# A new order of the same steps for a fused long convolution and feed-forward kernel

## The chip, the cores and the metric

The kernel runs on one core of a Trainium2 chip. The metric is device time in microseconds (us); the engines are PE (matmuls), DVE and ACT (elementwise work and copies out of PSUM), POOL and SP (here mostly queues that issue DMAs).

## The reference

```python
x = A_q                                   # (1, 2048, 640) bf16, as k and v
xn = layernorm(x)
k_shift = sum(k_pad[:, t:t+S] * shift_k[:, 3-t] for t in range(4))   # 4 taps
kv = k_shift * v
y = irfft(rfft(kv, 4096) * rfft(ssm_k, 4096))[:2048] + kv * ssm_D    # along the sequence
s = xn * y
g = silu(gelu(xn @ w1 + b1) @ w2 + b2)    # 640 -> 1728 -> 640
out = x + s * g
```

## The kernel before

The 2048 positions lie as 128 partitions by 16 rows of 640 channels. SBUF holds one pool, `mem`, of 111 rows of 128 x 640 bf16, and every intermediate result sits in rows that are given by number. PSUM's eight banks are given by number too.

The whole kernel is a list of some 990 short words, `PLAN`. Each word is one step: a name with its indices, then `/row` for where its result goes in `mem`, `@bank` for its PSUM bank (`@6.7` takes two), and `~a` or `~d` for the engine of a copy out of PSUM (ACT or DVE). The program runs through the words and emits each step's instructions; each engine, and each engine's DMA queue, then executes its own in the order of the words. Waits between engines are put in from the rows and banks that steps share. So the order on an engine is the order of the list, and a step that is not ready holds all that follows it there. At most eight DMAs of SP's queue are under way: each waits for the landing of the one eight places before it, and POOL's likewise.

The steps, with their lines:

- Feed-forward, in four chunks `c` of 512 positions: `st`, `rs`/`sq`, `nm` are the layer norm (L405 to L421); `tx`, `tt` turn x on PE (L426, L432) and `te` copies it out (L191 on ACT, L192 on DVE, as all steps with `~a` or `~d`); `ha`, `hb`, `h` are the first matmul (L451, five matmuls), `he` the gelu (ACT, L456); `g` is the second matmul (L466, 14 matmuls of 320 columns), `ge` the silu (ACT, L471), `gm` the product with xn (DVE, L475). `wu` and `wv` are matmuls on nothing that warm PE (L267).
- Convolution: both filter and kv go through a transform in two stages. Filter: `kt` turns it (L483), `kc` copies it out, `kf` is the first stage (two matmuls, L197), `ke` copies it out, `ks` stores it to DRAM as scrK (POOL, L496). kv: `cm`, `ca`, `cv` are the taps, their sum and the product with v (DVE, L502, L505, L508), `uf` the first stage (L197), `ue` its copy, `us` its store to scrU (POOL, L518). The stage between goes through DRAM, since it regroups the lines: `fl` loads from scrK (SP, L521; it needs all 16 `ks`), `ff` is the second stage in 32 x 32 pieces (L207), `fe` its copy, `mk` a copy with partitions swapped (SP, two DMAs, L532). `ml` loads from scrU (SP, L535; it needs all 16 `us`), `mu` is its second stage (L207), `mp` the product of the spectra (DVE, L544), `mc` and `md` the first inverse stage (L207), `me` its copy, `ms` the store to scrC (POOL, L558).
- Sine tables: `ws`, `ss` (ACT); `it` turns them (L563), `ie` copies them out.
- Last stage: `yl` loads from scrC (SP, L576; it needs all 16 `ms`), `y` is the last inverse stage (four matmuls, L583), `yc` its copy (ACT, L587), `yt` the gate (DVE, L592), `yo` adds x (DVE, L598), `os` stores the output (SP, L603).
- Input loads, all on SP: `xl` and `q` (x), `wa` (w1), `wb` (w2), `cl` (filter), `kl` and `klh` (k), `vl` (v).

Of the kernel before, what the change touches and what calls it, by code (L numbers as in the profile page):

```python
# [41 lines left out]
ca0_3 ks3 kt7@3 ge0_6/2 cm1_3/39 kt10@4 kc7/12~a kf5_1@6.7 kf5_0@0.1 cv0 kc10/60~a g0_3@5 gm0_6 ke5_0/63~d ke5_1~a
cm1_2/61 ks5 kt9@4 ge0_3/0 kt6@2 cm2_0/58 kc9/107~a kf7_0@0.1 kf7_1@6.7 ke7_0/6~a gm0_3 g0_5@3 ca1_1 kc6/14~a
cm3_0/85 ke7_1~a ca1_2 uf0_0@4.5 ks7 ge0_5/1 uf1_0@0.1 kt8@2 ue0_0/41~a cm2_1/101 uf1_1@6.7 g0_4@3 ue1_0/12~a ca1_3
ue1_1~a st2_1 us1 uf0_1@4.5 cv1 ge0_4/2 kf6_0@0.1 kf6_1@6.7 ue0_1~a st2_0 g0_2@3 kc8/110~a us0 ke6_0/4~a st2_3
ke6_1~a uf3_1@4.5 ca2_1 ge0_2/0 uf2_0@0.1 ks6 uf2_1@6.7 ue2_0/67~a kt11@2 cm2_2/61 kt12@3 ue2_1~a uf3_0@0.1 st2_2
# [5 lines left out]
h1_3@2 ke12_1~d ke14_0/0~a kc13/107~a it3@3 ca3_2 ks12 uf5_1@0.1 he1_3 kf13_0@4.5 cm4_0/39 h1_7@7 ue5_1~a ca3_3
ke13_0/108~a us5 kf13_1@0.1 ca4_1 he1_7 it2@6 kf15_0@4.5 ke13_1~a cv3 h1_12@2 ke15_0/6~a ks13 cm4_2/41 ie2/43~a
uf6_0@0.1 uf6_1@4.5 gm0_7 h1_4@7 cm4_3/12 ue6_0/19~a ue6_1~d ie3~a h1_10@6 cm5_1/21 us6 he1_4 uf7_1@0.1 cm5_0/23
uf7_0@4.5 he1_10 h1_9@3 ca4_2 ue7_0/25~a ue7_1~a ca5_1 kf15_1@6.7 kf14_1@4.5 he1_9 h1_8@0 us7 ca4_3 ke14_1~a
cm5_2/27 ke15_1~a h1_11@1 ks14 cv4 he1_8 ks15 h1_5@3 he1_12 ca5_2 he1_11 cm5_3/2 uf8_0@4.5 he1_5 uf9_0@6.7 cm6_2/4
# [25 lines left out]
gm2_0 me18/33~a ml14/51 mp19/12 mu20@2.3 mu24@6.7 he3_0 h3_4@5 mp20/103 mc19@0.1 md19 mp24/95 he3_4 mu22@2.3 h3_3@4
me19~a mp22/85 ms9 mc20@0.1 mu23@6.7 md20 he3_3 h3_13@5 me20/87~a mp23/59 mc21@2.3 mc22@0.1 md21 he3_13 md22 h3_8@4
me21~a me22/53~d ms10 mu31@6.7 mc23@2.3 he3_8 gm2_7 md23 mu28@0.1 h3_1@5 mp31/68 me23~a ms11 mc24@2.3 md24 mp28/39
he3_1 mu25@6.7 h3_12@4 me24/70~a mp25/72 mu27@2.3 mu26@0.1 h3_5@5 he3_12 mp26/27 mc25@6.7 md25 he3_5 h3_11@4 me25~a
mp27/31 ms12 mc26@0.1 mu29@6.7 md26 he3_11 h3_6@5 me26/85~a mp29/33 mc27@2.3 mu30@0.1 md27 he3_6 h3_2@4 me27~a
# [581 lines left out]
```

## Time and profile before

| | us |
|---|---|
| median of 3 runs | 208.4 (208.17 to 208.75) |
| profiled execution, its own time | 207.69 |
| its span (first to last instruction) | 205.9 |
| PE busy | 192.1 |
| DVE busy | 175.8 |
| ACT busy | 159.7 |
| POOL busy | 39.8 |

The span is what the profile's rows divide up; the time of the execution has 1.8 us around it. PE's granted clock was 1.00 throughout. PE's bounds are its own work and the idle time between: with 93% busy, the waits ahead of its matmuls tell more than its busy time. In a list of waits the columns are the total, how often, and the longest; in a chain, the start, the duration and what ran; in a timeline, start, duration, engine, line and operation.

### The profile page before, as it was taken

What the parts mean: (1) busy time and instruction counts of PE and PEld (TensorE: products, weight loads), DVE (VectorE), ACT (ScalarE), POOL (GpSimd) and SP (SyncE); (2) the same over time, 40 slices, a digit from 0 to 9 for tenths busy, and PEclk for the clock granted to TensorE, in tenths of its full rate; (3) what the DMA queues carried; (4) which work ended last, traced back from release to release, by engine and by line L of the source; (5) the groups of instructions that cost most, each with busy time, mean ns of one, the idle gap of its engine ahead of it and who ended that gap; (6) DMA issues with size and microseconds to landing.
All of it is one profiled execution on the core that took longest, in us unless ns stands there. A gap on an engine that the chain in (4) does not pass through costs nothing.

```text
span 205.9 us, 5536 instructions
## 1 busy us (share of the span) xinstructions
PE 192.1 (93%) x2194; PEld 114.1 (55%) x2194; DVE 175.8 (85%) x300; ACT 159.7 (78%) x246; POOL 39.8 (19%) x71
## 2 busy tenths in 40 slices
PE   2989999999989999999999999999999999999982
PEld 1576666677656655656753333566653333666750
DVE  8999559799999999999897797899799997036983
ACT  5899999568999999987799777754688767645760
POOL 8302003212361323210240002111221212100000
PEclk9999999999999999999999999999999999999999
DMA  6999999994454435699997999999971323599993
GB/s 223 371 411 295 361 363 416 410 426 176 191 199 183 172 149 193 184 381 400 316 351 251 309 378 371 368 357 394 338 241 43 131 81 119 173 302 389 337 338 121
DMA packets 27120, 57.71 MB, mean 280 GB/s; under 512 B 2966, under 2 KB 16983, under 8 KB 27094
## 3 DMA queue, kind: packets, MB, share of 16 engines
q1 hardware_dynamic: 23072, 41.62, 57.6%
q0 software_dynamic: 3840, 15.73, 19.8%
q8 instruction: 17, 0.28, 0.6%
q14 instruction: 9, 0.07, 0.1%
q10 hardware_dynamic: 182, 0.01, 0.1%
HBM read 33.76 MB, written 18.35 MB: 253 GB/s over the span
## 4 chain that ended last, share of the span: by engine, by line
PE 54%; DMA 18%; DVE 12%; ACT 11%; issue 3%; SPq 1%; ACTq 1%; DVEq 0%
PE ps L451 22%; PE ps L466 16%; DMA mem<-scrK 8%; PE ps L207 7%; DMA mem<-scrC 6%; PE ps L197 5%; DMA scrK<-mem 3%; DVE mem L502 3%; DVE mem L505 3%; DVE mem L192 2%; ACT mem L191 2%; ACT hT L456 2%; DVE stats L405 2%; ACT L456 1%; ACT mem L587 1%
## 5 line engine op out<-in xcount | busy, mean ns | idle before, releaser
L451 PE MATMUL ps<-mem,w_sb 128*128 128x512 bf16 (+1 forms) x310 | 69.1, 363 | 0.1
L466 PE MATMUL ps<-w_sb,hT 128*128 128x320 bf16 x448 | 66.0, 299 | 0.3 <-ACT mem L191 0.3
L191 ACT CAST mem<-ps 128x640 bf16<-128x640 f32 x94 | 62.3, 699 | 3.1 <-PE ps L207 1.6
L466 PEld LDWEIGHTS <-hT 128*128 128x128 bf16 x448 | 42.7, 98 | 19.2 <-issue 2.4
L544 DVE TENSOR_TENSOR mem<-ps,mem 128x1280 bf16<-128x1280 f32 x32 | 46.0, 1485 | 3.5 <-PE ps L207 1.7
L456 ACT ACTIVATE hT<-ps,b_f 128x512 bf16<-128x512 f32 (+1 forms) x56 | 37.3, 694 | 10.8 <-PE ps L451 10.4
L451 PEld LDWEIGHTS <-w_sb 128*128 128x128 bf16 x310 | 28.4, 99 | 27.8 <-issue 4.9
L192 DVE CAST mem<-ps 128x640 bf16<-128x640 f32 x34 | 27.6, 820 | 8.7 <-PE ps L207 3.0
L471 ACT ACTIVATE sl<-ps 128x320 bf16<-128x320 f32 x32 | 13.9, 438 | 21.2 <-PE ps L466 20.8
L502 DVE TENSOR_TENSOR mem<-mem 128x1280 bf16<-128x1280 bf16 x32 | 25.4, 818 | 1.2 <-DMA scrK<-mem 1.2
L197 PE MATMUL ps<-mem 128*128 128x320 bf16 x128 | 23.7, 299 | 1.4 <-ACT mem L191 0.7
L207 PE MATMUL ps<-mem,mats 32*32 32x320 bf16 x1024 | 22.8, 300 | 1.2 <-DMA mem<-scrK 0.4
L558 POOL DMA_DIRECT2D scrC<-mem x16 | 11.4, 716 | 59.3 <-ACT mem L191 32.6
L191 ACT COPY mem<-ps 128x640 bf16<-128x640 bf16 (+2 forms) x27 | 20.6, 783 | 1.5 <-PE ps L426 0.8
L207 PEld LDWEIGHTS <-mats 32*32 32x32 bf16 x1024 | 9.6, 88 | 17.7 <-issue 14.7
L505 DVE TENSOR_TENSOR mem<-mem 128x1280 bf16<-128x1280 bf16 x24 | 19.2, 810 | 0.0
L475 DVE TENSOR_TENSOR mem<-mem,sl 128x320 bf16<-128x320 bf16 x32 | 9.7, 318 | 8.2 <-ACT sl L471 8.2
L197 PEld LDWEIGHTS <-mem 128*128 128x128 bf16 x128 | 12.0, 98 | 8.3 <-issue 2.5
L496 POOL DMA_DIRECT2D scrK<-mem x16 | 9.1, 569 | 33.9 <-DVE mem L192 21.2
L518 POOL DMA_DIRECT2D scrU<-mem x16 | 8.7, 545 | 32.6 <-ACT mem L191 19.1
L405 DVE BATCH_NORM_STATS2 stats<-mem 128x6 f32<-128x320 bf16 x32 | 13.8, 474 | 0.0
L587 ACT CAST mem<-ps 128x640 bf16<-128x640 f32 x16 | 10.1, 705 | 2.0 <-PE ps L583 1.7
(75 smaller groups left out, 138.5 us busy)
## 6 DMA issues: line engine op xcount, KB each, us to landing
scrK<-mem POOLq DMA_DIRECT2D x16, 320.0 KB, 4.2
scrU<-mem POOLq DMA_DIRECT2D x16, 320.0 KB, 3.5
mem<-scrK SPq DMA_DIRECT2D x16, 320.0 KB, 4.3
mem<-mem SPq DMA_DIRECT2D x32, 160.0 KB, 5.5
mem<-scrU SPq DMA_DIRECT2D x16, 320.0 KB, 6.6
scrC<-mem POOLq DMA_DIRECT2D x16, 320.0 KB, 4.2
mem<-scrC SPq DMA_DIRECT2D x16, 320.0 KB, 6.2
mem<-in_A_q_dram SPq DMA_DIRECT2D x7, 640.0 KB, 7.5
```

Of the source, the lines that this page charges most:

```text
L191: return nc.scalar.copy(out=out_ap, in_=in_ap)
L192: return nc.vector.tensor_copy(out=out_ap, in_=in_ap)
L197: nc.tensor.matmul(out=o[:, h, :], lhsT=lhsT, rhs=rhs[:, h * HALF:(h + 1) * HALF], start=start, stop=stop)
L207: nc.tensor.matmul(out=o[j, h, :], lhsT=m[i, i], rhs=rhs[i, h * HALF:(h + 1) * HALF], start=start, stop=stop)
L405: nc.vector.bn_stats(out=stats[:, n, h, :], in_=x_row(n)[:, h * HALF:(h + 1) * HALF])
L451: nc.tensor.matmul(out=bank(hname(c, ft))[:, a:b], lhsT=w1_sb[:, t, ft * P:(ft + 1) * P], rhs=rhs, start=(t == 0), stop=(t == DT - 1))
L456: nc.scalar.activation(out=hT[0:M, ft, :], in_=bank(hname(c, ft))[0:M, :], func=ACT.Gelu_apprx_tanh, bias=b1_f[0:M, ft:ft + 1], scale=1.0)
L466: nc.tensor.matmul(out=bank(f"g{c}_{i}")[:, 0:HALF], lhsT=hT[0:M, ft, q * P:(q + 1) * P], rhs=w2_sb[0:M, ft, hs], start=(ft == 0), stop=(f ...
L471: nc.scalar.activation(out=at["sl", c, i], in_=bank(f"g{c}_{i}")[:, 0:HALF], func=ACT.Silu)
L502: nc.vector.tensor_tensor(out=rows(f"cm{i}_{j}", 2), in0=rows("kz0", 2, 3 + 2 * i - j), in1=taps(j), op=ALU.mult)
L505: nc.vector.tensor_tensor(out=rows(f"cm{i}_0", 2), in0=rows(f"cm{i}_0", 2), in1=rows(f"cm{i}_{j}", 2), op=ALU.add)
L544: nc.vector.tensor_tensor(out=rows(f"mp{g}", 2).rearrange("p k (h c) -> p k h c", h=2), in0=banks(f"mu{g}")[:, None, :, :].to_broadcast([P ...
```

## The change

The same steps stand in a new order. The new order was found by moves within the old one, judged over replays in which the lengths of transfers were varied. The list keeps every step; rows and banks are given out anew, 46 of the copies out of PSUM change between ACT and DVE, and the one step `wv2` (two warm-up matmuls) becomes `wv1` twice. No function changes. All 63 lines of the list differ; these are the ones with the steps that the prediction speaks of (the old lines, then the new ones):

```diff
-io1/0 dm qs xl0_0/8 xl0_1 id pd/12 cl0/19 wa0 cl4 qr xl1/35 wa2 w cl1 io2 wu@0 kz0/39 cl3 st0_0 ws1/58 cl2 mh st0_1
-klh pt@1 em0@2 pb sq0 em1@3 kz1 rc0 nm0_0 nm0_1 tx0@4 st0_2 tx1@5 wa1 te0_0/65~a wv2 st0_3 te0_1~a ee0/69~a wb0
-ha3@6 ee1~d ha0@7 sq1 ws2/73 rc1 ha2@1 nm0_2 nm0_3 ha1@0 wb1 st1_0 em3@4 tx2@5 em2@2 st1_3 tx3@3 st1_1 te0_3~a
-ws0/77 it1@3 kl0 te0_2~d st1_2 hb2 hb1 xl3/81 ee3~d he0_2 rs1 hb0 s it0@5 hb3 kl3 h0_12@4 he0_3 he0_0 kl2 h0_13@1
...
-ke0_0/61~d h0_7@0 kc2/63~a he0_12 kf2_0@6.7 tt1_0@1 he0_7 ke2_0/13~d xl2/15 kf1_1@2.3 vl2/93 h0_8@4 te1_0/97~d
-te1_1~a ke1_1~d kf0_1@6.7 he0_8 h0_9@5 vl1/0 cm1_1/4 ks1 ke0_1~a cm0_3/6 kt4@4 ks0 he0_9 kf2_1@0.1 kt3@2 cm0_1/101
...
-gm0_0 ge0_1/1 kf4_0@4.5 cm0_2/58 kf3_1@0.1 ke4_0/101~a kf4_1@6.7 g0_6@2 gm0_1 ca0_2 ke4_1~a ke3_1~a kc5/110~d ks4
...
-ue3_0/39~a kf8_1@6.7 us2 ca2_2 ue3_1~a rs2 kf8_0@0.1 ke8_0/63~a gm0_2 kf9_0@4.5 ke8_1~d ke9_0/108~a kf10_1@0.1 gm0_5
-kf10_0@6.7 kc12/14~a cm2_3/87 ks8 kf9_1@4.5 ke10_0/6~a us3 tt1_2@3 nm2_1 ca2_3 te1_2~a g0_7@6 ke9_1~a nm2_2 nm2_3
...
-uf8_1@0.1 h1_6@2 ue9_0/87~a ca5_3 ue8_0/47~a fl0/33 uf9_1@6.7 ue8_1~d fl10/107 he1_6 h1_13@3 fl6/31 ue9_1~a cv5
-fl2/29 us8 fl1/85 tt2_0@2 he1_13 us9 cm6_3/58 fl3/60 uf10_0@4.5 uf11_0@0.1 te2_0/62~a cm6_0/41 uf11_1@6.7 g1_2@3
...
-fl11/0 te2_1~a fe10/109~d us15 mk4/19 nm3_1 fe11~a nm3_3 nm3_0 mk5/58 ff14@6.7 ff5@4.5 ff18@0.1 ge1_7/2 nm3_2 h2_0@3
-fe14/33~a fe5~d fl8/41 fe18/60~a gm1_7 mk2/105 ff19@6.7 ff15@4.5 he2_0 h2_11@2 fe19~d fl13/103 fe15~d fl14/12
-ff21@0.1 ml0/23 ff20@6.7 ml2/53 he2_11 h2_9@4 fe20/55~d ml8/68 fe21~a ml7/101 ff22@2.3 ff24@6.7 he2_9 ff23@0.1
...
-h2_6@5 mk12/21 me1~d me2/95~a ms0 mc3@2.3 mc4@6.7 md3 he2_6 md4 mu5@0.1 h2_10@4 me3~d ml5/51 me4/87~a mp5/107 ms1
...
-me16/27~a ml12/19 tt3_1@4 te3_0/0~a mc14@0.1 md14 mp17/87 mc15@2.3 mk13/6 md15 me14/101~a tt3_2@5 me15~a mu18@0.1
...
-h3_10@4 me30/87~d me31~a h3_7@5 ms15 he3_10 he3_7 g3_2@4 yl15/21 g3_5@5 ge3_2/2 yl13/41 yl14/6 yl4/109 yl10/4
...
-yc11 yo12_1 g3_3@0 yl1/66 yo2 yc8 yt10 os2 yt11 yl6/68 yo10 yt8 y0@6.7 os10 ge3_3/0 yo11 y9@2.3 yc0 yo8 os11 y7@4.5
-gm3_3 os8 yc9 yt0 g3_0@1 yo13_1 yc7 yt9 os13 yo0 yt7 os0 yo9 y5@6.7 ge3_0/2 yo7 os9 y1@2.3 gm3_0 yc5 os7 yo12_0
-y6@4.5 yc1 os12 yt5 g3_6@0 yc6 yo5 yt1 os5 yt6 yo1 yo6 ge3_6/1 os1 os6 gm3_6 yo15_0 os15_0
+io1/0 dm qs xl0_0/8 xl1/12 id pd/16 xl0_1 wa0 wa2 qr cl0/23 cl1 w cl2 io2 wu@0 kz0/39 cl3 st0_0 ws1/58 mh cl4 st0_1
+pt@1 em0@2 wa1 pb sq0 em3@3 kz1 rc0 wv1 nm0_0 nm0_1 tx0@4 st0_2 tx1@5 te0_0/65~a em1@6 klh st0_3 te0_1~a wv1
+ee0/69~a ha2@7 ee1~d ha0@1 sq1 ws2/73 rc1 ha1@0 nm0_2 nm0_3 tx2@2 tx3@6 kl0 te0_2~d ha3@4 te0_3~d st1_0 hb3 wb0 hb2
+ws0/77 st1_1 hb1 h0_13@5 wb1 st1_3 h0_11@2 he0_1 st1_2 xl2/81 h0_10@6 s rs1 kl1 he0_11 h0_12@0 he0_3 he0_2 it0@2
+vl0/85 it1@4 he0_10 hb0 d he0_13 nm1_1 kt1@7 nm1_3 he0_12 kt0@6 nm1_2 em2@5 nm1_0 he0_0 vl1/89 kc1/58~d tt1_0@0
...
+ha4@4 he0_6 kc0/16~d ha5@3 cm0_2/63 hb4 kc2/17~d hb5 cm0_1/101 ke1_0/103~a kf0_0@6.7 h0_8@5 he0_5 cm0_0/105
...
+cm0_3/101 he0_7 kl3 kt3@1 kc8/58~d vl2/65 kt4@4 he0_9 kf2_1@6.7 sm kf0_1@2.3 ke2_1~a ca0_2 g0_0@5 kc3/39~a vl3/0
...
+ke7_1~a cm2_2/6 ge0_3/1 uf1_1@2.3 ks7 ca2_1 uf1_0@6.7 kf6_0@4.5 ks1 cm2_3/101 g0_2@1 ue1_0/63~a ue1_1~a ca2_2
...
+ke10_1~a kf11_1@4.5 uf4_0@2.3 he1_0 ke11_1~d h1_1@6 ue4_0/109~d ks11 kf12_0@0.1 uf5_0@4.5 ks0 ca3_2 kt13@2 he1_1
...
+he1_11 fl0/91 cm6_2/89 fl6/30 h1_13@2 he1_6 fl4/32 gm0_5 fl1/42 ue8_0/109~d uf8_1@4.5 fl3/6 he1_13 uf11_0@0.1 fl2/26
...
+ge1_6/0 cv7 ue12_1~a uf13_1@0.1 st3_2 ff6@4.5 us12 ff7@6.7 g1_3@2 ue13_1~a us11 fe6/22~a st3_0 us8 fe7~a us10 gm1_6
...
+rs3 uf15_1@4.5 ue15_0/0~d tt2_2@7 tt2_1@6 ue15_1~a ff10@2.3 te2_2~d ff11@0.1 ff8@4.5 te2_1~d g1_7@7 fe10/52~a us13
+gm1_1 fe11~a fe8/93~d us9 nm3_2 us15 nm3_3 ff9@2.3 ff14@0.1 ff5@4.5 nm3_0 ge1_7/1 h2_0@6 fe9~a fe14/2~d fe5~a
+ff18@2.3 ff20@0.1 he2_0 mk2/6 ff19@4.5 h2_11@7 fe18/105~d fe20/91~d fl13/54 ff15@2.3 mk4/89 fe19~d he2_11 ff21@0.1
+h2_9@6 fe15~a ml0/18 fe21~d ml2/109 nm3_1 ff24@4.5 ml1/79 ff23@2.3 ff22@0.1 he2_9 h2_5@7 fl15/77 fe24/75~d fe22/73~a
...
+mu28@4.5 mu31@0.1 md23 h3_1@2 mp28/105 ms0 me23~a ms2 he3_8 h3_5@6 mp31/109 he3_1 ms4 ms9 mu25@4.5 mc24@2.3 md24
...
+me31~a gm2_7 he3_9 h3_7@2 gm2_6 ms15 he3_10 he3_7 g3_4@3 yl15/6 g3_2@2 yl4/85 yl13/24 yl14/26 yl3/0 yl12/28 g3_5@0
...
+yc4 y14@4.5 yc13 yl5/4 yt4 g3_7@2 yt15 yc14 yo4 yl1/16 ge3_4/2 yt14 yt13 yl6/105 y3@6.7 gm3_2 gm3_4 ge3_7/0 y12@0.1
...
+yc7 yt0 os11 yt9 os15_1 yt7 yo9 y5@2.3 yo7 ge3_0/1 os9 y1@0.1 yo0 os8 yc5 gm3_0 y6@6.7 os0 yo13_1 yc1 yt5 os13
+g3_6@4 yc6 yo5 os7 yt1 os5 yt6 yo1 yo6 ge3_6/0 os1 os6 gm3_6 yo12_0 yo15_0 os15_0 os12
```

In the old order the stores `ks`, `us`, `ms` stand where their data is ready, and loads of scrK, scrU and scrC are spread among the steps that use them. In the new one many of the stores stand later (`ks1`, `ks0`, `ks2`; `us8`, `us10`, `us11`, `us13`, `us9`; `ms0` to `ms7`), and many loads earlier (`kl0` ahead of `wb0`; `fl4`, `fl8`, `fl12`, `fl14`; `ml9`, `ml14`, `ml15`; all `yl` ahead of all `os`). `yo12_0` and `os12` move to the very end.

More of the change, by code (lines that the diff above doesn't have):

```diff
@@ L42 @@
[L42 to L46, printed above, removed]
@@ L52 @@
[L52 to L56, printed above, removed]
@@ L82 @@
[L82 to L86, printed above, removed]
@@ new lines @@
+ke0_0/107~a cm1_0/109 kf2_0@0.1 h0_7@3 he0_8 cm1_1/18 ke2_0/20~a ca0_1 kt9@5 he0_4 kf1_1@6.7 h0_9@0 kc9/22~d ke1_1~a
+cm0_3/101 he0_7 kl3 kt3@1 kc8/58~d vl2/65 kt4@4 he0_9 kf2_1@6.7 sm kf0_1@2.3 ke2_1~a ca0_2 g0_0@5 kc3/39~a vl3/0
+cm1_3/4 ke0_1~a ca0_3 kt6@0 ge0_0/0 st2_3 kf3_0@6.7 g0_1@1 st2_1 ke3_0/6~a st2_0 kc4/40~a kt5@5 kt7@2 kc5/17~a
+kf3_1@6.7 g0_6@3 st2_2 kc6/16~a ge0_1/1 ca1_1 rs2 ke3_1~a cm1_2/63 kt10@4 ge0_6/2 kf4_1@0.1 kc10/41~a kf4_0@6.7 cv0
+g0_3@5 kc7/101~a ks3 nm2_2 nm2_3 ke4_0/18~a nm2_0 ke4_1~a ca1_2 kf5_0@2.3 kf7_0@6.7 kf5_1@0.1 ca1_3 ke7_0/39~a
@@ new lines @@
+g0_5@4 cv1 ke5_0/85~a ke5_1~a nm2_1 cm2_1/63 kf7_1@6.7 uf0_0@2.3 gm0_6 g0_4@0 gm0_1 ue0_0/4~a cm2_0/87 ge0_5/2
+ke7_1~a cm2_2/6 ge0_3/1 uf1_1@2.3 ks7 ca2_1 uf1_0@6.7 kf6_0@4.5 ks1 cm2_3/101 g0_2@1 ue1_0/63~a ue1_1~a ca2_2
+ke6_0/42~a us1 gm0_3 gm0_0 uf2_0@6.7 ge0_4/1 cm3_0/6 ks4 uf0_1@2.3 ge0_2/0 uf3_0@4.5 ks5 ue2_0/39~a ue0_1~d kt14@0
+kt15@1 ue3_0/105~a uf3_1@6.7 kc14/17~d kf6_1@2.3 kc15/44~d ue3_1~a kf8_0@4.5 gm0_2 kf8_1@0.1 ke8_0/103~a ke6_1~d
+kt11@6 kt12@7 ke8_1~a kc11/110~d kf9_0@4.5 uf2_1@2.3 ca2_3 kc12/16~a kf9_1@0.1 g0_7@6 ke9_0/63~a cv2 ke9_1~a
@@ new lines @@
+te2_0/101~a fl12/16 cm6_0/105 ue9_1~a cm7_0/18 fl9/20 ue10_0/87~a ca6_1 ff1@6.7 ff0@4.5 fl8/48 uf10_1@0.1 fe0/36~a
+g1_0@3 ca6_2 ge1_2/2 fl5/63 ue10_1~d cm7_1/22 ff12@4.5 ff13@0.1 fe1~a g1_6@2 cm6_3/67 ge1_0/1 ca7_1 fe12/107~a
+fe13~a gm1_0 ca6_3 ff2@6.7 ff3@4.5 ff4@0.1 mk6/95 g1_5@3 cm7_3/93 fe2/34~a fe4/28~a mk0/57 cv6 fe3~a cm7_2/91
+fl14/46 uf12_1@6.7 ge1_5/1 mk1/85 uf12_0@0.1 ca7_2 uf13_0@4.5 ue12_0/89~a g1_1@3 gm0_7 fl11/30 ca7_3 ue13_0/50~a
+ge1_6/0 cv7 ue12_1~a uf13_1@0.1 st3_2 ff6@4.5 us12 ff7@6.7 g1_3@2 ue13_1~a us11 fe6/22~a st3_0 us8 fe7~a us10 gm1_6
@@ new lines @@
+ml8/71 ml15/87 fe23~d ml3/63 ff17@4.5 ff16@0.1 h2_8@6 he2_5 fe16/65~d fe17~a ml5/42 ff28@2.3 ff25@0.1 ff26@4.5
+h2_2@7 ml7/26 fe28/32~d fe25~a he2_8 fe26/50~d ml11/67 mu0@0.1 ff27@2.3 h2_1@6 mp0/4 fe27~a ml4/20 he2_2 mu4@4.5
+ff29@2.3 h2_13@7 mk3/0 mp4/24 fe29~a he2_1 ml13/69 mu2@0.1 mc0@2.3 md0 mp2/44 mu1@4.5 h2_3@6 me0/30~a ml14/48 he2_13
+mp1/16 h2_7@2 ml9/54 he2_3 ml10/46 mu3@0.1 ff30@6.7 h2_4@3 mp3/56 fe30/18~a mk5/4 he2_7 mc2@4.5 mc1@6.7 md2 md1
+h2_6@2 ml6/36 me2/79~d me1~a he2_4 gm1_4 mk7/34 mc3@0.1 gm1_3 mc4@6.7 md3 gm1_7 md4 mu5@4.5 h2_10@3 me3~d me4/85~a
@@ new lines @@
+md13 mk10/52 mu16@4.5 g2_0@3 mp16/26 te3_0/2~a me13~a gm2_4 mc16@0.1 mu17@4.5 md16 ge2_0/0 mc14@6.7 md14 mp17/34
+tt3_1@2 me16/71~a me14/26~a tt3_2@3 mc15@0.1 md15 te3_2~a te3_1~d mu18@6.7 mc17@4.5 md17 me15~a mp18/16 q1/34
+mu21@2.3 me17~a g2_7@0 ms8 mp21/65 ms3 mc18@4.5 mu20@6.7 ms7 md18 gm2_0 h3_0@1 mp20/77 ge2_7/0 ms5 me18/53~a ms6
+mu19@2.3 mu24@4.5 h3_4@0 he3_0 mp19/46 ms1 h3_3@6 mp24/16 he3_4 mc19@2.3 he3_3 mu22@0.1 md19 mp22/71 me19~a mc20@4.5
+mu23@6.7 md20 me20/91~a h3_13@2 mp23/28 mc21@4.5 mc22@0.1 md21 he3_13 md22 h3_8@3 me21~a me22/26~d ms10 mc23@6.7
```

49 lines of the change are left out of this document (21 added, 28 removed).

## Prediction

> **What bounds the kernel now.** I read the page's sections 1 and 2, then PE's waits, the chain, and the timelines of DVE and SP where the chain leaves PE.
>
> ```profile
> span 205.9 us, 5536 instructions
> PE 192.1 (93%) x2194; PEld 114.1 (55%) x2194; DVE 175.8 (85%) x300; ACT 159.7 (78%) x246; POOL 39.8 (19%) x71
> ...
> DMA  6999999994454435699997999999971323599993
> ```
>
> The profiled execution took 207.69 us, 1.77 beyond its span; the median of the runs is 208.4, 0.71 more. A matmul of 320 columns takes 0.136 us in the chain (14 of L466 in 1.90), and PE has the same 2194 matmuls in both orders, so of the 205.92 us span only 13.86 of PE idleness can change. PE's timeline places it: 3.71 before the first matmul, 4.12 after the last (201.80), 6.03 between. This 6.03 (2.9%) is all that a new order can remove there. The DMA row (40 slices of 5.15 us) is full up to 46 us, from 87 to 149 and from 180 to 200: three stretches where one transfer more delays the next.
>
> PE's waits (total, times, longest us):
>
> ```profile
> PE ps L267 <- POOL ident masks.py:199: 3.7, 1, 3.7
> PE ps L583 <- DMA mem<-scrC: 1.2, 3, 0.5
> PE ps L563 <- ACT mem L191: 0.8, 1, 0.8
> PE ps L197 <- ACT mem L191: 0.7, 4, 0.2
> PE ps L483 <- DVE mem L192: 0.6, 1, 0.6
> PE ps L207 <- DMA mem<-scrK: 0.4, 1, 0.4
> ```
>
> By place: 1.74 up to 26 us (0.08, 0.41, 0.78, 0.47); 1.80 from 40.8 to 59.1 (0.63 ahead of kt7, then six of 0.16 to 0.28 up to g0_7); 1.32 from 92 to 151 (0.43 ahead of ff3, 0.35 ahead of mu0, 0.28 around mu18, two of 0.13); 1.17 in the last stage (0.40, 0.25, 0.52, ahead of y4, y3, y6).
>
> The chain shows where the second group comes from:
>
> ```profile
> 30.47 1.42 DVE mem L192 x2
> 31.89 0.30 issue
> 32.19 7.02 DMA scrK<-mem
> 39.23 0.82 DVE mem L502
> ```
>
> The product cm0_2 writes rows 58 and 59, where ke1 lies until the store ks1 has left it. ks1 is issued at 32.18 into full DMA engines and lands 7.0 us later. From there the chain runs on DVE without a break to 57.9, DVE being busy 19.83 of the 20 us from 39.2 to 59.2. So these 1.80 us are DVE's lateness.
>
> **Part 1: first 26 us; take +0.9 of the 1.74.** The 0.78 was it1, whose bank waited for te0_3 on ACT, queued behind sq1 and the sine ws2. Now te0_3 is on DVE (0.4 to 0.8 us by the rows of L192 COPY), and it0 and it1 stand after four ffn1 steps: gone. One of two warm-up matmuls (0.43 each here) fills the 0.41 ahead of tx0, but the other, with em1, no longer reaches to te0_1 (9.90), so about 0.2 and 0.35 stay. The 0.47 was kf1_0 waiting for the bank of he0_11; kf1_0 now has other work ahead of it. Left: about 0.85. Bounds: all 1.74 gained; 1 us lost if hb3, which now follows te0_3 directly, waits for both DVE copies.
>
> **Part 2: 26 to 60 us; take +1.3 of 1.80.** kl0 goes ahead of the 2080 KB of wb0 on SP, and the stores ks0, ks1, ks2 are moved to a point 17 to 30 us of PE work later. Products start before those stores, cm0_2 in rows 63 and 64, so the 1.24 us that DVE waited at 39.2 goes, and its 3.07 idle us between 25 and 30 get work. Evacuations change engine: 9 ke go from DVE to ACT and 2 back, 8 kc from ACT to DVE and 1 back. Spaced as in the chain (f32: DVE 0.73, ACT 0.59; kc on DVE 0.40, on ACT 0.59), that is 7 x 0.73 less and 7 x 0.40 more, so 2.3 us off DVE, even on ACT. ACT's load up to g0_7 falls by 1.5 us by the same spacings, DVE's stays, with less idleness before it. DVE should be ahead, not late; I keep 0.5 for steps in another order. Bounds: 0 and 1.80.
>
> **Part 3: 60 to 178 us; take +0.2 of 1.32.** Loads of scrK come forward (fl8, fl12, fl14 by 15 to 21 us of PE work), ml9, ml14, ml15 by 25 to 40, and the stores ms0 to ms7 leave the full stretch for 150 to 165, where DMA digits are 1 to 3: 8 x 320 KB. That should end the 0.28 at mu18 (ml9) and the 0.13 at ff30. fl1 is fourth instead of fifth in its queue and the stores us8 and us9 leave its side, which covers the 0.43. Against it stands the scrU hand-over. SP before:
>
> ```profile
> 104.98 2.62 SPq L532 DMA_DIRECT2D mem<-mem  x4
> 107.72 0.51 SPq L521 DMA_DIRECT2D mem<-scrK  x1
> 108.33 1.92 SPq L532 DMA_DIRECT2D mem<-mem  x2
> 110.70 0.87 SPq L521 DMA_DIRECT2D mem<-scrK  x2
> 111.82 3.44 SPq L535 DMA_DIRECT2D mem<-scrU  x6
> ```
>
> us15 was issued at 104.67 and landed 3.7 us later (108.4); ml0 started only at 111.82, since SP stood before it at swaps that waited for ACT and DVE. So us15 had 3.4 us to spare. Now us13 and us9 stand right ahead of us15 on POOL, two more issues of 0.54 and two more stores in its queue, so it starts about 0.7 later and takes between 3.7 and 7.0 us (the worst store into scrU): 109.1 to 112.4. SP has only mk2, fl13 and mk4 ahead of ml0. I take a 0.8 us wait at mu0, near the early end, since fewer loads run beside it and the 3.7 us came with DMA digits at 9; its bounds are 0 and 2.9 (112.4 plus the 5.0 from ml0 to mu0, against PE at 114.5). The Trainium skill (DMA: Bandwidth & Descriptors, Queues, rings and completion order) says that an engine takes turns between the queues it has work for, packet by packet; by that, POOL's three stores, 0.98 MB at half of some 390 GB/s, would need about 5 us, an estimate that lies inside these bounds and makes the wait about 1.
>
> **Part 4: the last stage; take +1.0 of 1.17.** Before, yl6 was issued at 193.09, behind stores that waited for DVE on SP, and landed 6.04 us later; y6 waited. Now all 16 yl stand ahead of the first os, in the order of the y steps, and y15 comes one ffn2 group (1.9 us) later. y6 has 9.8 us of PE work after its load's place, before 4.6; y4 waited for the fourth load, and the fourth load now serves y14, 0.5 us later. Bounds 0 and 1.17.
>
> **Part 5: after the last matmul; take -0.7.** yo12_0 now stands between gm3_6 and yo15_0 (0.24 on DVE), and os12 follows os15_0 on SP (0.33), as a whole row (3.6 us to landing against 3.2 for a half). 0.24 + 0.33 + part of 0.4. Bounds -0.3 and -1.0. Nothing covers this.
>
> **Sum.** 0.9 + 1.3 + 0.2 + 1.0 - 0.7 = 2.7 us: 207.69 becomes 205.0 in a profile, and 208.4 becomes 205.7. I say 205.8. The ends: all bounds on the good side 208.4 - 1.74 - 1.8 - 1.32 - 1.17 + 0.3 = 202.7; on the bad side 208.4 + 1 + 2.9 - 0.35 + 1.0 = 213.0, neither likely as a whole.
>
> **Rivals.**
>
> 1. The scrU hand-over is the late one: us15 lands at 112.4 and mu0 waits 2.9 instead of 0.8. Then 207.9. For it: its place behind us13 and us9. Against: the lighter load beside it. Chance 0.18.
>
> 2. Slower: DVE stands at cm0_2, waiting for kl0, with kc2 and kc8, evacuations that kf2_0 and kf8 need, behind it. DVE gets there at about 27 us. By the bytes ahead of it (7116 KB with its own) and the GB/s of slices 1 to 5 (223, 371, 411, 295, 361 by 5.15 us), kl0 is in at 22. But the loads of A_k took 11.8 us from issue, and in the old order the first product ran at 31.8. Every us after 27 goes to PE; past 30 the gain is gone, at 31.8 the price is 4.8: 210.5. Chance 0.21.
>
> 3. The late clock. PE's rows show 256-column matmuls 0.213 apart up to 11.6 us and 0.109 from there. The turn came 3.73 us after the end of the last early gap (7.86). The gap now expected before ha2 ends at 9.95; if the turn counts from there it comes at 13.7, 2.1 us later, half of them lost: 1.05, and 206.9. Chance 0.08. The Trainium skill (TensorE: Matmul & The Clock Gate, section on the HAM clock gate) has half rate until a window of about 3.4 us was busy, with windows that run freely, not from the last gap; by that the turn may come in either order at the same time, and the trace's 3.73 fits both.
>
> 4. The removed waits return one step on, DVE and PE being full together from 40 to 90: 208.4, give or take 0.8. Of steps with under 0.9 us of PE work between the matmuls that fill a bank or row and those that need it, I count 15 in the old order and 10 in the new, which speaks against. Chance 0.06.
>
> **The numbers.** Forecast 0.47, its own range 203.8 to 207.7. Something under 0.3% (0.6 us) is what the measurement can't tell from no change; the three runs of before spread by 0.58 us. Faster: 0.45 of the forecast, 0.08 of rival 1, 0.07 of rival 3, 0.60. Same: 0.02 + 0.08 + 0.01 + 0.03 = 0.14. Slower: rival 2 with 0.21, 0.02 of rival 1, 0.03 of rival 4: 0.26. The range 203.8 to 210.3 leaves out the far half of rival 2 and the best ends.
>
> **What would show it.** PE idle between its first and last matmul near 2.6 us instead of 6.0; no 7 us store in the chain near 32; DVE's first product before 29; no wait of L583 on scrC; the tail after the last matmul near 4.8. The forecast is wrong if DVE's waits show L502 on the load of A_k for over 2 us, or PE's waits L207 on scrU for over 2.

## The result, and the profile after

The new order takes 201.56 us (median of four runs, 201.33 to 201.93), the old one 208.37 in the same comparison: a ratio of 0.9673, with a 95% interval of 0.9652 to 0.9694, or 6.8 us less. The forecast was 2.7 less. The direction was right; the size was wrong by a factor of 2.5, and 201.56 lies below the range. The profiled execution took 201.33 us (before: 207.69). Here and below, medians are of all executions, while the ratios leave out those more than 1.5% above the fastest of the same kernel, so a ratio can differ by some tenths of a per cent from that of the medians.

The page of the new order, span, busy times and DMA row:

```profile
span 199.5 us, 5511 instructions
PE 189.4 (95%) x2194; PEld 114.7 (57%) x2194; DVE 175.7 (88%) x304; ACT 155.1 (78%) x242; POOL 39.9 (20%) x71
...
DMA  5999999982607979999967999997868492599983
```

PE's matmuls are the same 2194, but PE's busy time fell from 192.1 to 189.4. That is the first surprise: 2.7 of the 6.4 us of shorter span are not in PE's idle time at all.

PE's waits of 0.15 us or more (total, times, longest us), the whole list:

```profile
PE ps L267 <- POOL ident masks.py:199: 3.7, 1, 3.7
PE ps L359 <- DMA prm<-in_A_ssm_D_dram: 0.4, 1, 0.4
PE ps L451 <- ACT mem L191: 0.2, 1, 0.2
PE ps L207 <- DVE mem L544: 0.2, 1, 0.2
PE ps L451 <- DVE mem L192: 0.2, 1, 0.2
```

Between its first and last matmul PE is idle for 1.30 us instead of 6.03. No wait on scrK, scrU or scrC is left. In the old chain, ks1's store took 7.02 us up to 39.2, and the chain then ran on DVE. In the new chain, this stretch is PE's own work (start, us, what ran):

```profile
30.37 1.08 PE ps L451 x5
31.45 0.62 PE ps L483 x10
32.07 0.54 PE ps L197 x4
32.61 1.90 PE ps L466 x14
```

By section 4 of the two pages, PE's share of the chain went from 54% to 86%, that of DMA from 18% to 2%, and that of DVE from 12% to 3%:

```profile
PE 86%; ACT 3%; issue 3%; DVE 3%; DMA 2%; ACTq 1%; DVEq 0%
```

SP's queue around the scrU hand-over (start, us, engine, line, operation):

```profile
103.21 1.76 SPq L532 DMA_DIRECT2D mem<-mem  x2
105.06 0.54 SPq L521 DMA_DIRECT2D mem<-scrK  x1
105.74 1.10 SPq L532 DMA_DIRECT2D mem<-mem  x2
107.58 1.62 SPq L535 DMA_DIRECT2D mem<-scrU  x3
```

ml0 goes out at 107.58, us15 had been issued at 100.33 (and landed at 104.88), and mu0 starts at 111.14 without a wait.

**Where the 6.4 us lie.** I took the distance from each matmul's start to the next one's and subtracted what the columns need (0.136 us for 320 columns at full clock). What is left over is what a wait costs PE. Each distance counts in the stretch in which it starts:

| stretch | before, us | after, us |
|---|---|---|
| matmuls at half clock, beyond what full clock takes | 3.33 | 2.54 |
| waits up to 26 us | 2.69 | 1.60 |
| 26 to 62 us | 3.39 | 0.60 |
| 62 to 176 us | 3.57 | 2.52 |
| last stage, from 176 us | 1.72 | 0.03 |
| last matmul's end to the span's end | 4.12 | 5.15 |

The differences are 0.79, 1.09, 2.79, 1.05, 1.69 and -1.03: 6.38 of the 6.39 us. The largest is the 26 to 62 us stretch. The two engines that copy out of PSUM look as follows there. Before, then after (for each stretch its length, then the busy us of PE, PEld, DVE, ACT and POOL, PE's clock, DMA share, GB/s):

```profile
26.00:53.00 27.00, 26.37 (x213) 18.99 (x212) 23.62 (x39) 21.82 (x38) 5.11 (x9) 1.00 0.89 350
53.00:62.00 9.00, 7.82 (x58) 5.08 (x57) 8.93 (x21) 8.95 (x17) 4.99 (x8) 1.00 0.51 196
```

```profile
26.00:53.00 27.00, 27.00 (x217) 19.70 (x216) 26.43 (x52) 24.49 (x43) 5.58 (x8) 1.00 0.82 315
53.00:62.00 9.00, 9.00 (x67) 5.89 (x66) 8.93 (x13) 8.86 (x15) 2.13 (x5) 1.00 0.18 67
```

In the old order, both copying engines are full from 53 us on (8.93 and 8.95 of 9), and PE waits for them. Before 53 they stood idle for 3.38 (DVE) and 5.18 us (ACT). The new order does 2.81 us more on DVE and 2.67 more on ACT between 26 and 53. From 53 on they are just as full there (8.93 and 8.86), but PE, which has other steps between the copies' matmuls, does not wait. In this stretch PE gains 2.79.

### The profile page after: what moved, and what is told of

The parts are those of the page before. It is cut to its first block, busy times and chain, and to the rows that moved or that the text cites. A ratio compares the mean times of both kernels' runs of the same rounds, so it can differ in the third digit from the quotient of the medians.

```text
span 199.5 us, 5511 instructions
## 1 busy us (share of the span) xinstructions
PE 189.4 (95%) x2194; PEld 114.7 (57%) x2194; DVE 175.7 (88%) x304; ACT 155.1 (78%) x242; POOL 39.9 (20%) x71
## 4 chain that ended last, share of the span: by engine, by line
PE 86%; ACT 3%; issue 3%; DVE 3%; DMA 2%; ACTq 1%; DVEq 0%
PE ps L466 30%; PE ps L451 29%; PE ps L197 9%; PE ps L207 7%; PE ps L583 4%; PE ps L483 3%; ACT mem L191 2%; DMA prm<-in_A_ssm_D_dram 2%; PE ps L432 1%; DVE mem L544 1%; DVE mem L192 1%; PE ps L563 1%; PE ps L351 1%; ACT L471 1%; ACT sl L471 0%
## 5 line engine op out<-in xcount | busy, mean ns | idle before, releaser
L191 ACT CAST mem<-ps 128x640 bf16<-128x640 f32 x101 | 67.0, 699 | 13.8 <-PE ps L207 10.2
L451 PE MATMUL ps<-mem,w_sb 128*128 128x512 bf16 (+1 forms) x310 | 67.8, 359 | 0.4 <-ACT mem L191 0.2
L502 DVE TENSOR_TENSOR mem<-mem 128x1280 bf16<-128x1280 bf16 x32 | 25.1, 821 | 0.0
L192 DVE CAST mem<-ps 128x640 bf16<-128x640 f32 x27 | 21.7, 821 | 3.0 <-PE ps L207 1.7
L207 PE MATMUL ps<-mem,mats 32*32 32x320 bf16 x1024 | 22.6, 300 | 0.4 <-DVE mem L544 0.2
L197 PE MATMUL ps<-mem 128*128 128x320 bf16 x128 | 22.7, 299 | 0.0
L207 PEld LDWEIGHTS <-mats 32*32 32x32 bf16 x1024 | 9.8, 88 | 15.9 <-issue 13.5
L191 ACT COPY mem<-ps 128x640 bf16<-128x640 bf16 (+2 forms) x16 | 11.4, 746 | 1.7 <-DVE mem L544 0.8
L192 DVE COPY mem<-ps 128x640 bf16<-128x640 bf16 (+2 forms) x21 | 11.4, 578 | 0.3 <-PE ps L426 0.3
```

The costliest lines, as they stand in the source:

```text
L191: return nc.scalar.copy(out=out_ap, in_=in_ap)
L192: return nc.vector.tensor_copy(out=out_ap, in_=in_ap)
L197: nc.tensor.matmul(out=o[:, h, :], lhsT=lhsT, rhs=rhs[:, h * HALF:(h + 1) * HALF], start=start, stop=stop)
L207: nc.tensor.matmul(out=o[j, h, :], lhsT=m[i, i], rhs=rhs[i, h * HALF:(h + 1) * HALF], start=start, stop=stop)
L451: nc.tensor.matmul(out=bank(hname(c, ft))[:, a:b], lhsT=w1_sb[:, t, ft * P:(ft + 1) * P], rhs=rhs, start=(t == 0), stop=(t == DT - 1))
L502: nc.vector.tensor_tensor(out=rows(f"cm{i}_{j}", 2), in0=rows("kz0", 2, 3 + 2 * i - j), in1=taps(j), op=ALU.mult)
```

## The experiments

The yardstick in each group is the kernel before on the same chip; its median was 209.0 to 209.2 us there. "Waits" below are PE's, as in the table above. Steps are shown one group of words per line.

**1. The new order once more.** No edit.

> The new order once more, unchanged, as the yardstick of this group of runs and as a test of how far one profile of it speaks for all. If the waits that went are the order's doing, its ratio to the kernel before is again 0.965 to 0.970, TensorE stands less than 1.5 us between its first and last matmul (1.3 in the first profile), and no matmul of the 26 to 62 us stretch waits on scrK or on kl0. If the 6.4 us of shorter span owed part to a lucky set of transfer lengths, the ratio is above 0.975 and a wait of a us or more for a transfer (L207 or L197) is back. The turn of the clock to full speed, at 9.49 us in the first profile, may lie anywhere between 7.3 and 12.4 us, as it did over the profiles so far; 1 us of it is worth 0.5 us of time.

Measured: 201.88 us, ratio 0.9646 (0.9596 to 0.9696). The waits of 26 to 62 us are again 0.60 (this trace lacks 19 of the 2194 matmul records, and the distances across them are taken as two). The clock turned to full speed at 11.76 us instead of 9.49 and half rate cost 3.49 instead of 2.54; the span is 200.4, which is 0.9 longer. So the waits that went belong to the order. That the 0.79 us of clock in the table do is not shown: at the old order's turn (11.59) the new one has 5.5 us less span, not 6.4.

**2. The new order with the old engines** for the 46 copies.

```diff
-te0_3~d kc0/16~d kc2/17~d ke1_0/103~a ke0_0/107~a ke2_0/20~a
+te0_3~a kc0/16~a kc2/17~a ke1_0/103~d ke0_0/107~d ke2_0/20~d
...
```

> The new order, with the 46 copies out of PSUM put back on the engines that they had in the old order (ACT or DVE); nothing else differs. Theory A: in the stage from 26 to 62 us the change of engines takes 2.3 us off DVE, and without it PE waits there again, 1.0 to 2.5 us: 202.6 to 204.1. Theory B (rival): the early start of the products and the postponed stores leave DVE enough room, and the engines of the copies hardly count: at most 0.6 more than the new order, 201.4 to 202.2.

Measured: 215.38, ratio 1.0315 (1.0264 to 1.0366). Both theories missed: the price is 13 to 14 us. Waits of 26 to 62 us: 5.79. ACT did 19.07 us of work between 26 and 53 (new order: 24.49), DVE 24.51.

**3. The old order with the new engines.**

```diff
-te0_3~a ke1_0/59~d kc0/12~a ke0_0/61~d kc2/63~a ke2_0/13~d
+te0_3~d ke1_0/59~a kc0/12~d ke0_0/61~a kc2/63~d ke2_0/13~a
...
```

> The old order, with the 46 copies out of PSUM on the engines that the new order gives them; nothing else differs. Theory A: the choice of engines is a gain by itself (2.3 us off DVE in the crowded stage), so the waits from 40 to 59 us shrink: 0.5 to 2 us less than before, ratio 0.990 to 0.998. Theory B (rival): engines and order only fit each other, as the 14 us show that the new order lost with the old engines; in the old order the new engines give new waits: 1 to 10 us more, ratio 1.005 to 1.05.

Measured: 214.27, ratio 1.0257 (1.0198 to 1.0317). DVE did 20.06 us between 26 and 53 (before: 23.62); waits 5.31. Each choice of engines is worse in the other's order, by 5 and by 13 to 14 us: the choice is no part that can be priced alone, and the "2.3 us off DVE" of the forecast's Part 2 was such a price.

**4. Stores straight behind their copies**, in the new order (40 of the `ks`, `us`, `ms` moved).

```diff
 ke1_1~a
+ks1
...
 ks7 ca2_1 uf1_0@6.7 kf6_0@4.5
-ks1
...
```

> The new order, with each store to scrK, scrU and scrC (ks, us, ms) put straight behind the copies that make its data, as the old order has them; 40 of the 48 move. Theory A: the stores were postponed out of the full stretches of the DMA engines, and at their old places they hold up loads: waits of PE on scrK, scrU or scrC come back, 1 to 3 us: 202.5 to 204.6. Theory B (rival): what counted was that no product writes rows that a store still reads; the place of the stores does not matter: within 0.5 of the new order, 201.1 to 202.1.

Measured: 203.71, ratio 0.9745 (0.9696 to 0.9795), against 0.9646 to 0.9673 of the new order: some 1.5 to 2 us. The hand-overs wait again:

```profile
PE ps L207 <- DMA mem<-scrK: 1.1, 1, 1.1
PE ps L207 <- DMA mem<-scrU: 0.5, 1, 0.5
```

The waits of 26 to 62 us stay at 0.61. So the late stores are a part of its own. POOL's timeline tells how they may pay, at their old places and then in the new order:

```profile
80.37 1.22 POOL L518 DMA_DIRECT2D scrU<-mem  x2 [5.55 <-DVE mem L475]
82.54 0.54 POOL L518 DMA_DIRECT2D scrU<-mem  x1 [0.96 <-ACT mem L191]
85.13 0.54 POOL L518 DMA_DIRECT2D scrU<-mem  x1 [2.04 <-DVE mem L192]
```

```profile
74.71 1.07 POOL L518 DMA_DIRECT2D scrU<-mem  x2
93.13 1.07 POOL L518 DMA_DIRECT2D scrU<-mem  x2 [17.34 <-ACT mem L191]
```

fl2 is issued at 80.01 here and at 80.03 in the new order. Here four stores of 320 KB to scrU go out beside it, and it takes 9.1 us to land; in the new order none does, and it takes 6.3. ff4, which needs it, starts at 89.13 instead of 87.71. That these four stores are the whole cause is likely, but no run moved them alone.

**5. k's load late**, in the new order.

```diff
 te0_0/65~a em1@6
-klh
...
 tx2@2 tx3@6
-kl0
...
 wb1
+klh kl0
 st1_3
```

> The new order, with the loads of k that the first products need (klh and kl0) put behind the 2080 KB of w2 (wb0, wb1) in SP's queue, as the old order has them. Theory A: the first product, at 25.4 us in the new order, waits until about 31, and DVE holds the copies kc2, kc9 and kc8 behind it, so PE stands for 2 to 5 us: 203.5 to 206.5. Theory B (rival): PE has other work and DVE makes it up: within 0.6: 201.2 to 202.2.

Measured: 206.84, ratio 0.9892 (0.9836 to 0.9948), some 5 us of the gain gone, most of it in one wait; DVE's waits from 20 to 36 us give its cause:

```profile
PE ps L197 <- DVE mem L192: 4.5, 1, 4.5
```

```profile
DVE mem L502 <- DMA mem<-in_A_k_dram: 4.9, 1, 4.9
```

This is the rival of the slower side, made to happen. DVE stands at cm0_2 until kl0, issued at 20.55, is in at 30.1; kc2 stands behind it, and kf0_0 waits. Its price was put at 4.8, and the wait cost 4.6 by spacing (in the profile a stretch at half clock comes on top of it; see the last section). In the new order as it is, DVE's first product runs at 25.37, earlier than the forecast had DVE get there (27).

**6. kl0 first**, in the old order.

```diff
 ee0/69~a
+kl0
 wb0
...
 it1@3
-kl0
```

> The old order, with kl0 (the first 640 KB of k) ahead of the 2080 KB of w2 (wb0) in SP's queue; nothing else differs. Theory A: the early k is what lets DVE start its products and run ahead, so here too the first product starts some us earlier than 31.8 and the waits from 40 to 59 us shrink by 1 us or more: ratio 0.990 to 0.996. Theory B (rival): the products stand behind copies on DVE in the old order, and cm0_2 still waits for ks1, so the early load alone brings nothing: ratio 0.997 to 1.002, or more where w2 comes late for g0_0.

Measured: 210.21, ratio 1.0056 (1.0012 to 1.0099). The first product still starts at 31.65: DVE's five copies stand ahead of it. Waits of 26 to 62 us 3.35, and 2.3 us at scrK:

```profile
PE ps L207 <- DMA mem<-scrK: 2.3, 1, 2.3
```

**7. kc5 ahead of cm0_2**, in the old order.

```diff
 kf4_0@4.5
+gm0_1 kc5/110~d
 cm0_2/58
...
```

> The old order, with gm0_1 and kc5 on DVE ahead of cm0_2, the product that stands 1.24 us until the store ks1 has landed. Theory A: the waits from 40 to 59 us come from this one stop of DVE: the 0.80 us ahead of kt7 go, and DVE is 0.64 us earlier from there on, which shortens the seven later waits too: 0.8 to 1.6 us less, ratio 0.992 to 0.997. Theory B (rival): DVE is short of time by itself in this stage, and what kt7 gains is given back up to 59 us: at most 0.4 less, ratio 0.998 to 1.001.

Measured: 209.24, ratio 0.9985 (0.9937 to 1.0033). kt7's wait (0.63 us, the largest of the stretch) is gone; kf10_0 waits 0.89 instead, and scrK takes 3.0. The stretch keeps 3.13, although DVE did 0.51 us and ACT 0.71 us more between 26 and 53 than before.

**8. The last six `yl` together**, in the old order, behind yl9.

```diff
 yl9/33
+yl8/0 yl0/2 yl7/85 yl5/87 yl1/66 yl6/68
 y4@4.5
...
```

> The old order, with the last six loads from scrC (yl8, yl0, yl7, yl5, yl1, yl6) ahead of all stores of the output in SP's queue, as in the new order; the y steps keep their order. Theory A: y3 and y6 no longer wait for scrC, while y4, whose load does not move, does: of the 1.65 us from start to start that these three cost, 1.1 go: ratio 0.993 to 0.996. Theory B (rival): the full DMA engines carry the same bytes, the stores of the output land later, and the end of the program moves by as much as PE gains: ratio 0.998 to 1.002.

Measured: 208.93, ratio 0.9975 (0.9923 to 1.0027), between the theories. In the profile y6's wait is gone and the last stage's waits are 1.33 instead of 1.72.

**9. The early moves together**, in the old order: experiments 6 and 7, and three products ahead of three copies.

```diff
+cm1_1/4
 ke1_0/59~d
...
+cm0_3/6
 ke0_0/61~d
...
+cm0_1/101
 ke2_0/13~d
...
```

> The old order with three early moves made together: kl0 ahead of wb0 on SP's queue; cm1_1, cm0_3 and cm0_1 on VectorE ahead of ke1_0, ke0_0 and ke2_0; gm0_1 and kc5 ahead of cm0_2. Alone, kl0 gave 1.0056 and kc5 0.9985. Theory A, that the waits of the 26 to 62 us stretch go only when transfer and products are moved together: these waits fall from 3.39 us to about 1, the first product starts before 28 us in place of 31.79, and the ratio is 0.985 to 0.993. Theory B, that what is won there is given back at the hand-over over scrK, as in the single moves (2.3 and 3.0 us of wait at L207): ratio 0.997 to 1.002, with 2 us or more of waits on scrK.

Measured: 208.31, ratio 0.9943 (0.9909 to 0.9977). The first product now starts at 24.47 instead of 31.79, and the waits of 26 to 62 us are still 3.32. DVE's waits between 26 and 53 us show why, before and here:

```profile
DVE mem L192 <- ACT hT L456: 2.2, 1, 2.2
DVE mem L192 <- PE ps L197: 1.8, 2, 1.0
DVE mem L502 <- DMA scrK<-mem: 1.2, 1, 1.2
```

```profile
DVE mem L192 <- PE ps L197: 2.1, 3, 1.6
DVE mem L192 <- ACT hT L456: 1.4, 1, 1.4
DVE mem L475 <- ACT sl L471: 0.5, 1, 0.5
DVE mem L502 <- DMA scrK<-mem: 0.4, 1, 0.4
```

The store's wait fell from 1.2 to 0.4, but the copies now reach DVE before PE has filled their banks. From the start of the span to 53 us DVE did 45.58 us of work, hardly more than the 45.33 of before (between 26 and 53: 23.07 and 23.62, as the first product now lies ahead of 26). Moving products forward mostly moved DVE's idle time. At scrK another 1.8 us is given back.

**10. The later hand-overs repaired as well**: experiments 8 and 9 together, te0_3 on DVE, and fl1 ahead of fl2 and fl10.

```diff
 fl0/33 uf9_1@6.7 ue8_1~d
-fl10/107
 he1_6 h1_13@3 fl6/31
+fl1/85
...
 fl3/60
+fl10/107
...
```

> The same early moves in the old order, and with them the three hand-overs behind them: the scrK transfers in the order fl0, fl6, fl1, fl2, fl3, fl10, the last six yl transfers ahead of the os stores, and te0_3 on VectorE. Theory A, that the new order's gain is the sum of a few local repairs that fit together: the early gain is kept past scrK and the last stage loses its 1.3 to 1.7 us of waits; ratio 0.975 to 0.988. Theory B, that the gain needs the many other moves (copies between engines, stores pulled forward) as well: waits return at scrK or scrU, ratio 0.993 to 1.002.

Measured: 206.80, ratio 0.9892 (0.9846 to 0.9938), between the theories. scrK's wait is gone (fl1 is issued at 83.63 and ff3 starts at 92.23) and the last stage keeps 0.85. The 26 to 62 us stretch keeps 3.34, with 23.14 us on DVE up to 53. So a third of the gain can be had from local repairs, and that stretch is what they don't reach. One repair did not work alone: with te0_3 on DVE in the old order, PE still waited at it1, for 2.6 us here and 1.3 in experiment 13, against 0.78 before.

**11. g0_7 ahead of the run of filter stages**, in the old order. From 55 to 59 us six waits of 0.16 to 0.28 stand ahead of kf8_1 to g0_7; here the 1.9 us of g0_7 are put ahead of them, and kt12 into their midst.

```diff
 kt11@2 cm2_2/61
+g0_7@3
-kt12@3
...
 gm0_2
+ge0_7/0
 kf9_0@4.5
+kt12@3
...
 te1_2~a
-g0_7@6
...
```

> The old order with one move on TensorE: the 14 matmuls of g0_7 (with ge0_7, the ScalarE step behind them) go ahead of kt12 and of the run kf8_1, kf8_0, kf9_0, kf10_1, kf10_0, and kt12 goes into that run. Theory A, that TensorE gives out this run of filter stages faster than ScalarE and VectorE copy it out: 1.9 us of work put ahead of it lets the copies catch up, the six waits from 55 to 59 us (2.16 us in spacings) fall to 1 or less, the waits of the 26 to 62 us stretch from 3.39 to 1.5 to 2.3, and the ratio is 0.991 to 0.997. Theory B, that the copying engines are late by their load alone: the waits move to the stages behind the run, the stretch keeps 3 us or more, ratio 0.998 to 1.002.

Measured: 210.92, ratio 1.0078 (1.0031 to 1.0125). Worse than either theory: the waits rose from 3.39 to 5.08, of which 1.9 are one wait of kf11_0 for a copy on ACT. From 53 to 62 us:

```profile
53.00:62.00 9.00, 6.12 (x49) 4.17 (x47) 8.86 (x20) 7.48 (x14) 4.12 (x7) 1.00 0.45 172
```

ACT did 7.48 us of work instead of 8.95. While PE ran g0_7, ACT had nothing to copy, and the time it lost there came back on PE.

**12. A run of filter stages in the new order**: g0_7 behind kf11_0, kf10_1 and kf10_0.

```diff
 kf9_1@0.1
-g0_7@6
...
 kf10_1@0.1 kf10_0@2.3
+g0_7@6
 ke11_0/85~a
+ge0_7/0
...
```

> The new order with one move on TensorE: g0_7 (and ge0_7) behind kf11_0, kf10_1 and kf10_0, so that kf9_0, uf2_1, kf9_1, kf11_0, kf10_1, kf10_0 stand in a row as the filter stages do in the old order. Theory A: the waits of the 26 to 62 us stretch rise from 0.60 to between 1.3 and 2.5 us, and the time by 0.4 to 1.5, a ratio of 0.967 to 0.972 where the new order's is 0.965. Theory B, that the copying engines have time in hand in the new order: the waits stay under 1 us, ratio within 0.002 of the new order's.

Measured: 203.95, ratio 0.9772 (0.9718 to 0.9826). The waits are as theory A has them, 2.16 instead of 0.60, with 0.76 us shown ahead of kf11_0; the median is above A's range (the profiled execution took 202.59), though the interval reaches into it. Up to 53 us both copying engines did what they do in the new order (26.54 and 24.45 us from 26 on); over 53 to 62 us both fall back:

```profile
53.00:62.00 9.00, 7.91 (x58) 4.95 (x57) 7.38 (x11) 7.14 (x12) 0.84 (x2) 1.00 0.06 24
```

**13. Experiments 10 and 11 together.**

> The old order with all the repairs of b7 (0.9892) and the move of d1. Theory A: the run's waits go as well and no later hand-over takes them back; the 26 to 62 us stretch falls from 3.34 to 1.5 to 2.3 and the ratio to 0.980 to 0.986. Theory B: they return behind the run or at a hand-over through DRAM, ratio 0.987 to 0.992.

Measured: 208.10, ratio 0.9981 (0.9934 to 1.0028): the move of experiment 11 loses here too, with the same 1.90 us wait of kf11_0 and waits of 4.29 in the stretch. That is theory B's side, and worse than B had it. The clock is probably a part of this: the profiled execution took 209.40 with one fall to half clock in mid-kernel and a mean granted clock of 0.990; the four executions at 0.998 or more took 206.62 to 207.78, the six below 0.993 took 207.59 to 211.55. So how much the move alone costs here stays open.

**14. The tail**, in the new order.

```diff
 gm3_0
+yo12_0 os12
 y6@6.7
...
 gm3_6
-yo12_0
 yo15_0 os15_0
-os12
```

> The new order, with yo12_0 and the store os12 put back ahead of the last groups (behind gm3_0), so that only yo15_0 and os15_0 follow the last matmul. Theory A: the time after the last matmul falls from 5.1 to about 4.2 us as in the old order: 0.6 to 1.0 less, 200.5 to 201.0. Theory B (rival): the end is set by the landing of a store whichever it is, and by the end of the program: at most 0.3 less, 201.2 to 201.6.

Measured: 202.12, ratio 0.9671 (0.9624 to 0.9719), no different from the new order. In its profile the time behind the last matmul is 4.50 us instead of 5.15, but ha2 waited 0.60 (0.17 in the new order's first profile) and mu24 0.24, so that the last matmul ended 0.56 later.

**15. The tail, and `wv1` directly behind `wu`.**

```diff
 wu@0
+wv1
 kz0/39
...
```

> The new order with two local moves: the matmuls wv1 directly behind wu (TensorE stands less before pt, which waits 0.39 us for its transfer), and the copies yo12_0 and os12 behind gm3_0 at the end. Theory A, that what is left is the wait before pt and the time behind the last matmul: 0.4 us less at the start, and the time after the last matmul 4.5 us in place of 5.13, together 0.5 to 1.0 us, a ratio to the new order of 0.995 to 0.998. Theory B, that pt's wait only hides other work and that the tail is set by the last store's landing, which differs by more from run to run than the move is worth: within 0.2% of the new order in this same group.

Measured: 201.13, ratio 0.9614 (0.9566 to 0.9662), against 201.88 for the new order in the same group. The 0.75 us fits theory A (pt no longer waits, 4.4 us behind the last matmul), but the intervals of the two overlap: the best version by its median, not shown to be faster.

## Why the prediction was wrong in size

**The step that failed** is in the first part: "so of the 205.92 us span only 13.86 of PE idleness can change", and "This 6.03 (2.9%) is all that a new order can remove there." It took PE's busy time for fixed work. It is not, as a row of the new order's page shows:

```profile
L466 PE MATMUL ps<-w_sb,hT 128*128 128x320 bf16 x448 | 65.8, 299 | 0.2
```

The record of one matmul lasts 299 ns, yet the next one starts after 136. When PE has to wait, the last record runs on for 163 ns, and this counts as busy. Each wait is therefore about 0.16 us longer than the list of waits shows: kt7's 0.63 was 0.80, and kf8_1's 0.16 was 0.33. For the many short waits of the old order this is half of the price. A wait below 0.16 us doesn't show at all. Half-rate matmuls are in the busy time too. The Trainium skill (Perfetto Trace Analysis, Identifying the Most-Contended Engine) says that matmul occupancy is not a good measure of how close TensorE is to its roofline, because matmuls are pipelined. The trace agrees that it misleads: 2.69 us less busy with the same 2194 matmuls.

Of the 3.7 us that the forecast of 2.7 misses in the span, 1.9 were waits hidden in busy time and 0.8 half-rate matmuls, both outside what it counted; 1.3 were shown waits that it expected to stay; the tail took 0.3 back.

Point by point, in the spacings of the table:

- **Part 1** (0.9 forecast): the waits brought 1.09. it1's and kf1_0's went, as said; pt waits 0.39 for its transfer, ha2 and hb3 0.17 and 0.15. That it1's wait went because te0_3 is on DVE does not hold by itself (experiment 10). The clock added 0.79, which the repeat did not show (experiment 1): luck.
- **Part 2** (1.3 forecast): 2.79. This is the term most mis-sized. The mechanism ("So these 1.80 us are DVE's lateness") was half of it: of the seven waits in the old order, five, 1.0 of the 1.80 us, were for copies on ACT:

```profile
PE ps L197 <- ACT mem L191: 0.7, 4, 0.2
PE ps L483 <- DVE mem L192: 0.6, 1, 0.6
PE ps L466 <- ACT mem L191: 0.3, 1, 0.3
PE ps L197 <- DVE mem L192: 0.2, 1, 0.2
```

In experiments 7 and 9 DVE's wait for the store shrank and kt7's went, and the stretch kept 3.13 and 3.32. What fits better is that DVE and ACT are both full from 53 us, so that time in which they stood idle before is missing there. The forecast had one of those numbers in hand ("its 3.07 idle us between 25 and 30 get work") and priced the part by PE's 1.80 us of shown waits instead. Where the copying engines did less work (19.07 on ACT in 2; 20.06 on DVE in 3; 7.48 on ACT in 11; 7.38 and 7.14 in 12), the waits were 5.79, 5.31, 5.08 and 2.16; where they did about as much as before (9, 10), the waits were as before. This is a balance and not yet a cause: a copying engine that stands idle may itself be waiting for PE, as in 11. And it is not the whole: in 12 both engines did their full work up to 53, and the order of PE's own steps behind it brought 1.56 us of waits back. How the 2.79 divide between the two was not measured.
- **Part 3** (0.2 forecast): 1.05. The 0.8 charged for mu0 was not paid: it waits for nothing. Shown waits fell by 0.85. The rest may be the fewer changes between 128-row and 32-row matmuls (78 instead of 86); no run tried that alone.
- **Part 4** (1.0 forecast): 1.69, the right mechanism. Its three shown waits, 1.17, were 0.56, 0.41 and 0.68 in spacings, 1.65 in all.
- **Part 5** (-0.7 forecast): -1.03, at the far end of its bounds. Undoing its cause gave back 0.65 in experiment 14.

**Rivals.** Of the scrU wait (rival 1) there was none. Rival 2's mechanism is real and its price nearly right (experiment 5), but k was in time. Rival 3 gave the clock's turn at 13.7 us; it came at 9.49, and at 11.76 in the next profile. Over eight profiles of the new order and its variants it lay between 7.43 and 11.76, over nine of the old between 7.17 and 12.45. The Trainium skill (TensorE: Matmul & The Clock Gate, The HAM clock gate) has windows of about 3.4 us that run freely and a turn that varies from run to run; these numbers agree, though their spread of 5 us is wider than the 500 ns either way that the section gives. My "if the turn counts from there" falls: in the new order the gap ahead of ha2 ends at 10.10, behind the turn. Rival 4 is what the experiments found, not for the change as a whole but for its parts: made alone in the old order (3, 6, 7, 8, 11), they gave between 0.9975 and 1.0257. Why the many other moves fit together as they do was not taken apart further.

Of the signs, four came as said: no 7 us store near 32, the first product at 25.4, no wait of L583 on scrC, no long wait of L502 or of L207 on scrU. PE's idle time was forecast near 2.6 and was 1.30; the tail was forecast at 4.8 and was 5.15.

## What to carry to other kernels

Price a wait of PE by the spacing of matmul starts, not by the list of waits: each is longer by what a pipelined record hides, and many short ones double. Where two engines are full behind a stretch in which they stood idle, ask how much of that idle time on both the change fills; the waits that PE shows there do not bound the gain. Distrust a local repair: most of those tried here moved that idle time on, or had it taken back at the next hand-over. Choice of engine and order belong together: what an edit to one of them brings alone need not be its part in the pair.
